# Two PSUM pools, other homes for the normalised tokens and token sums, and later places for chunk 0's down weights and chunk 2's normalisation, in a fused spectral mixer and GEGLU kernel

## The chip, the cores and the metric

The kernel runs as one program on one core of a Trainium2 chip. The metric is the device time of one execution in microseconds (us); lower is better. Five engines appear in the profile: TensorE (PE for matmuls, PEld for its weight loads), VectorE (DVE), ScalarE (ACT), GpSimd (POOL), and SyncE (SP), which issues the DMAs. [...]

## The reference, cut to what matters

```python
# x: 8192 tokens x 448; mod rows from silu(c) @ w_mod
sa, ca, ga, sb, cb, gb = ...
h = layernorm(x) * (1 + ca) + sa
x = x + ga * irfft2(softshrink(mlp2(rfft2(h))))   # complex MLP, block-diagonal (4 blocks of 112), relu between
h = layernorm(x) * (1 + cb) + sb
x = x + gb * ((gelu(h @ w_gate) * (h @ w_up)) @ w_down)   # w_gate, w_up: 448 x 1792; w_down: 1792 x 448
```

The Fourier transform runs along the 8192 tokens (the other transformed axis has length 1). All inputs and outputs are float32.

## The kernel before, in words

The program has three stages. Up to about 80 us it loads x, normalises it and does the first part of the transform. Up to about 372 us it does the rest of the transform, the block MLP and most of the inverse transform, and writes the result to a DRAM buffer `vd`. From there to the end it runs the last step of the inverse transform, the second normalisation and the feed-forward network (FFN), in 32 **chunks** of 256 tokens. The change lies in this third stage.

**Precision.** The large matmuls work in fp16, each operand as a high and a low half: ACT writes the high half (a cast or scaled copy), DVE or POOL the rest (`..._hi`, `..._lo`). Matmuls are grouped in Strassen-like products, for which sums of tokens, weights and activations are formed.

**Chunks 0 to 7, the standard chunks** (372 to 768 us). The 1792 hidden columns are 14 tiles. The loop over a chunk i runs k = 0 to 13, and `gate_up(i, k)` issues gate and up matmuls of tile k (line L1125), then gelu on ACT (L1161), the product of both on DVE (L1166, `x<-pgu,gel`), and at odd k four sums on POOL (L1174 to L1177, `sums`). `quantize` (L1185 on ACT, L1186 on DVE) makes the fp16 pair `ac` from it, one or two k later. After k == 2 of chunk i, `down(i-1)` runs: seven products of matmuls (L1198 to L1200), two banks in turn, with an epilogue on ACT, DVE and POOL (L1225 to L1245) between them; L1226 writes the first quarter of the output buffer `o`, and L1234 reads the bank that the next product but one needs. `down` has three places (`mid`, 0 to 2) at which other steps are put in.

**What a chunk needs beforehand.** For chunk i: the loads of `v` (from `vd`), `g` and the residual `xx`; `split_g`/`split_v` (POOL, ACT); `inverse` (PE, L1026); `residual` (DVE L1035, and L1036 on DVE up to chunk 2, on POOL from chunk 3); `stats2` (DVE, L1044); `rsqrt_part`, small DVE steps; `norm2(i, b)` for b = 0 and 1 (DVE, L1074 and L1075), which writes the normalised tokens `n` in a buffer `n2`; `pack_hi` (ACT, L1080) and `pack_lo` (POOL for i > 0, L1087 to L1089) into the buffer `pk`; and `transposes_dma` (SP, L1095), transposing DMAs from `pk` to `nt`, which the matmuls read. For chunk 0 PE transposes (L1107).

**Weights made meanwhile.** `down_hi(t)` (ACT, L947) and `down_lo(t)` (DVE, L951, two instructions) make the seven pairs `wd` of down weights from float32 loads (`load_d8`); pair 1 ahead of chunk 0's loop, pairs 2 to 6 inside it. During chunks 0 to 7 the weight forms of the later chunks are made too (L1532 to L1580).

**Chunks 8 to 31, the units** (768 us to the end). Each chunk is seven units u = 56 to 223. `period(u)` issues stages a to d of four units in flight (L1360), with copies out of PSUM on ACT (`copy_b`, L1388, `sb<-set`) and DVE steps. Between stage a of unit u and its stage b, PE waits for `copy_b`. A unit's matmuls write one of three sets of two PSUM banks. For chunk 8 and later, `token_sums` (DVE L1301 to L1307 and one copy on POOL, L1303) forms sums of `n` in a buffer `tf`, which `wpack_hi` (ACT, L1331) and `wpack_lo` (POOL, L1337) pack into `pk`; `wtransposes` then transposes. In the first units of chunk 8 the list `opening` gives the steps of chunk 9.

**The order of the work** is written by hand. Dictionaries name steps to be issued after `gate_up(i, k)`: `hooks` for chunks i < 6, `soon` for i = 6 and 7, `second` for chunk 2's preparation in chunk 1, `ahead` and `first` for single places (key i * 14 + k), `prep` for the weight forms.

**PSUM.** In the standard chunks one pool of eight banks holds four tags of two: `pc` (inverse, transposes of chunk 0, and one product of down), `pa`, `pb` (gate and up), `pd` (down). After chunk 7 the pool is closed and another opened, with the three sets and two banks for down; set0, which unit 56 uses, lies on the former banks of `pc`.

**SBUF homes.** The pool `cp` is opened for the third stage. Its first tiles are wd1 to wd6, then two x1 tiles, then `pk`; `n2` comes after further tiles. `o` (tag "o") is one buffer of the pool `cq`; token sums of chunk 8 use this same tag. `x8()` gives one of three buffers with the products of a tile pair.

Of the kernel before, what the change touches and what calls it, by code (L numbers as in the profile page):

```python
# [10 lines left out]
F32 = mybir.dt.float32  # L11
F32R = mybir.dt.float32r
F16 = mybir.dt.float16
# [6 lines left out]
D = 448  # L20
# [4 lines left out]
CB = 2  # L25
# [13 lines left out]
NXT = 25  # L39
LA = 2  # L40
NSTD = 8
# [8 lines left out]
def spectral_geglu(ctx, tc, x, w1, b1, w2, b2, wg, wu, wd, cvec, wmod, cf1, cs2, cmi, cgm, out):  # L50
# [11 lines left out]
    wk = [[dram.tile([128, 2, 2, 2, b - a, 128], F16, name=f"wk{t}{a}") for a, b in WPARTS] for t in range(NP)]  # L62

    cpool = ctx.enter_context(tc.tile_pool(name="cpool", bufs=1))
    pctx = ExitStack()
    psum = pctx.enter_context(tc.tile_pool(name="psum", bufs=2, space=bass.MemoryType.PSUM))

    def bank(tag, name):
        return psum.tile([128, 512], F32, tag=tag, name=name)

    eps = cpool.tile([128, 1], F32, name="eps")
    V.memset(eps, EPS)
# [254 lines left out]
    with ExitStack() as bctx:  # L327
# [617 lines left out]
        def down_hi(t):  # L945
            for r, k in zip(draws[t], (slice(0, 3), slice(3, 7))):
                S.activation(wds[t][:, 0, k], r, AF.Copy, scale=dsc[:, t : t + 1])  # L947
# [32 lines left out]
    with ExitStack() as cctx:  # L980
        cp = cctx.enter_context(tc.tile_pool(name="cp", bufs=1, side="right"))
        H = 128 * CB
        wds = wds + [cp.tile([128, 2, 7, HC], F16, name=f"wd{t}") for t in range(len(wds), NP)]
        x1s += [cp.tile([128, CB, D], F32, name=f"x1{n}") for n in (1, 2)]
        pkt = cp.tile([128, NXT * 128], F16, name="pk")
        pkts = [pkt]
        nts, acts, pgu, outs = {}, {}, {}, []

# [79 lines left out]

        def norm2(i, b):
            mvt, x1, r = nxt[i]["mv"], x1t[i], nxt[i]["r"][0]  # L1070
            if b == 0:
                nxt[i]["n"] = cp.tile([128, CB, D], F32, tag="n2", name="n2")
            n = nxt[i]["n"]
            V.scalar_tensor_tensor(n[:, b], x1[:, b], mvt[:, b, 0:1], cb_r, op0=ALU.subtract, op1=ALU.mult)  # L1074
            V.scalar_tensor_tensor(n[:, b], n[:, b], r[:, b : b + 1], sb_r, op0=ALU.mult, op1=ALU.add)  # L1075
# [215 lines left out]
        def token_sums(i, part):  # L1291

            n = nxt[i]["n"]
            if part == 0:
                nxt[i]["t"] = cq.tile([128, 2 * D], F32, tag="o", name="tf") if i < NSTD + 1 else cp2.tile([128, 2 * D], F32, tag="tf", name="tf")
            t = nxt[i]["t"]
            b11, b21, x0 = n[:, 0, 0:192], n[:, 0, 192:384], n[:, 0, 384:448]
            b12, b22, x1 = n[:, 1, 0:192], n[:, 1, 192:384], n[:, 1, 384:448]
            t1, t2, t3, t4 = (t[:, o : o + 192] for o in (0, 192, 384, 640))
            if part == 0:  # L1300
                V.tensor_tensor(t1, b12, b11, ALU.subtract)  # L1301
                V.tensor_tensor(t3, b22, b12, ALU.subtract)
                G.tensor_copy(t[:, 576:640], x1)  # L1303
            else:
                V.tensor_tensor(t2, b22, t1, ALU.subtract)
                V.tensor_tensor(t4, b21, t2, ALU.subtract)
                V.tensor_tensor(t[:, 832:896], x0, x1, ALU.subtract)  # L1307
# [197 lines left out]
            6: [(2, wpack_hi, [4]), (2, wpack_lo, [4]), (3, load_g)],  # L1505
        }

        def pack(i):
            pack_hi(i)
            pack_lo(i)  # L1510
# [122 lines left out]
        for n, k in enumerate((4, 7, 11, 13)):  # L1633
# [17 lines left out]
            0: [(inverse,), (residual,)],  # L1651
            1: [(stats2,), (rsqrt_part, 5)],
            2: [(rsqrt_part, 9)],
            "down": [(norm2, 0), (norm2, 1)],
            "down2": [(pack_hi,), (pack_lo,), (transposes_dma, range(1))],
        }

        soon = {
# [6 lines left out]
            9: [(2, rsqrt_part, 5)],  # L1665
            10: [(2, rsqrt_part, 9)],
            11: [(2, norm2, 0)],
            12: [(2, norm2, 1)],
        }

        ahead = {
# [2 lines left out]
        }  # L1674

        first = {
            0: [(down_hi, 2), (down_lo, 2), (load_d8, 4)],
            2: [(inverse, 1), (residual, 1), (stats2, 1), (rsqrt_part, 1, 9)],
            3: [(down_hi, 3)],
            4: [(pack_hi, 1), (pack_lo, 1), (down_lo, 3), (load_d8, 5)],  # L1680
            6: [(down_hi, 4)],
            7: [(down_lo, 4), (load_d8, 6)],
            9: [(down_hi, 5)],
            10: [(down_lo, 5)],
            12: [(down_hi, 6)],
# [30 lines left out]
        S.copy(gb_r, gb[:, :D])  # L1716
        for t0 in range(0, 7, 2):
            transposes(0, t0)
        down_hi(1)
        down_lo(1)  # L1720
        load_d8(3)
        V.tensor_scalar(gb_r, gb_r, ds_d, None, op0=ALU.mult)

        def store_out():
# [5 lines left out]
            return bank("pc" if q == 1 else "pd", "pdn")  # L1730

        def steps_std(i, n):
            for fn, *args in second[("down", None, "down2")[n]] if i == 1 and n != 1 else []:
                fn(2, *args)
            for fn, *args in prep.pop((i, f"m{n}"), []):
                fn(*args)

        for i in range(NSTD):
            if i == 1:
                cctx2.close()  # L1740
                cctx2 = ExitStack()
                cp2 = cctx2.enter_context(tc.tile_pool(name="cp3", bufs=1))
            for k in range(NFT):
                gate_up(i, k)
                for fn, *args in ahead.pop(i * NFT + k, []):
                    fn(*args)
                if k % 2 == 1 and i + k > 1:
                    quantize(*((i, k // 2 - 1) if k > 1 else (i - 1, NP - 1)))
                if i == 1:
                    for fn, *args in second.get(k, []):  # L1750
                        fn(2, *args)
                for fn, *args in prep.pop((i, k), []):
                    fn(*args)
                if k == 2 and i > 0:
                    down(i - 1, two_banks, lambda n: steps_std(i, n))
                    if i == 1:
                        transposes_dma(2, range(1, 2))
                if k == 4:
                    store_out()
                for fn, *args in first.pop(i * NFT + k, []):  # L1760
                    fn(*args)
                if (i, k) in ((0, 3), (1, 1)):
                    load_v(i + 2)
                    load_g(i + 2)
                if i == 1 and k == 3:
                    split_g(3)
                    split_v(3)
                if k == 9 and i > 0:
                    load_v(i + 3)
                    load_g(i + 3)  # L1770
                for d, fn, *args in (hooks if i < NSTD - 2 else soon).get(k, []):
                    if i == NSTD - 2 and k < 3 and d == 1:
                        continue
                    if i + d > 2 and i > 0 and (i, k) != (1, 1):
                        fn(i + d, *args)
        quantize(NSTD - 1, NP - 1)
        assert not prep and not first and not ahead
        cctx2.close()
        pctx.close()
        cp2 = cctx.enter_context(tc.tile_pool(name="wp", bufs=1))  # L1780
        psum2 = cctx.enter_context(tc.tile_pool(name="psum2", bufs=1, space=bass.MemoryType.PSUM))
        sets = [psum2.tile([128, 2, 512], F32, name=f"set{n}") for n in range(3)]
        sets = [sets[(n - U0) % 3] for n in range(3)]
        pdn = [psum2.tile([128, 512], F32, name=f"pdn{n}") for n in range(2)]
        pkts.append(cp2.tile([128, NXT * 128], F16, name="pk2"))
        x1s.append(cp2.tile([128, CB, D], F32, name="x13"))

        opening = {
            0: [
                (2, split_v),  # L1790
                (1, token_sums, 0),
                (1, token_sums, 1),
                (1, wpack_hi, [0, 1]),
# [105 lines left out]
```

## Time and profile before

| What | Value |
|---|---|
| median of 3 runs | 1904.54 us (1901.68 to 1906.47) |
| profiled execution | 1902.93 us |
| its span, from first to last recorded work | 1901.1 us |
| mean granted TensorE clock | 0.993 |
| DMA moved | 330.49 MB |

The page of the profile gives busy times per engine for the whole span. A line of a timeline gives the start, the duration, engine, source line, operation, "out<-in" with the shapes, and in square brackets the idle time of the engine just before, with what ended it. "x2" behind a line means that two instructions of the kind are taken together. A line of the waits gives the total, the number and the longest. PEclk is the clock granted to TensorE, 1.00 being full speed.

### The profile page before, as it was taken

The numbers are of one execution on the slowest core, as the hardware profiler recorded it, in microseconds if no ns is written. First come the engines' busy times: TensorE is split into PE (matmuls) and PEld (weight loads), VectorE is DVE, ScalarE is ACT, GpSimd is POOL, SyncE is SP. The second block draws the span as 40 slices with busy tenths as digits, with TensorE's granted clock in tenths as the row PEclk, the third lists the DMA queues.
The fourth block names the chain that finished last, engine by engine and source line by source line (L and its number), as shares of the span: only waits on it lengthen the run. The fifth ranks groups of instructions, "written<-read, shape, count | busy, mean of one in ns | idle before, by whom it ended". The sixth has DMA issues, their size and how long they took to land.

```text
span 1901.1 us, 56363 instructions
## 1 busy us (share of the span) xinstructions
PE 1855.4 (98%) x23332; PEld 1756.8 (92%) x23332; DVE 1428.5 (75%) x2888; ACT 996.1 (52%) x1844; POOL 1266.1 (67%) x1616
## 2 busy tenths in 40 slices
PE   7899999899999999999999999999999999999998
PEld 3599999878898998899999999999999999999998
DVE  8677788778766666677777777777777777777645
ACT  5687888653444444344555545455455454444443
POOL 3157654257777777577777777777777777777533
PEclk9999999999999999899999999999999999999999
DMA  9999777645444445866666656556666666666651
GB/s 353 317 295 260 205 177 197 181 136 143 103 102 102 102 102 119 252 171 178 177 177 172 167 167 167 167 167 167 172 177 175 169 174 178 173 177 174 155 152 55
DMA packets 380602, 330.49 MB, mean 174 GB/s; under 512 B 110772, under 2 KB 358712, under 8 KB 380344
## 3 DMA queue, kind: packets, MB, share of 16 engines
q1 hardware_dynamic: 380344, 326.87, 62.4%
q8 instruction: 183, 3.00, 0.6%
q14 instruction: 75, 0.61, 0.1%
HBM read 243.32 MB, written 60.10 MB: 160 GB/s over the span
## 4 chain that ended last, share of the span: by engine, by line
PE 78%; DVE 11%; DMA 4%; ACT 2%; POOL 2%; SPq 2%; issue 1%; ACTq 0%; DVEq 0%; POOLq 0%
PE set L1360 34%; PE pgu L1125 11%; PE pdn L1198 6%; PE pdn L1200 6%; PE pdn L1199 6%; PE set L1198 2%; PE set L1200 2%; PE set L1199 2%; PE ps L210 2%; DMA xt<-in_A_x 2%; DVE y L471 1%; DVE x L1413 1%; DMA raw<-in_B_w_up 1%; DVE c L1397 1%; DVE wk L826 1%
## 5 line engine op out<-in xcount | busy, mean ns | idle before, releaser
L1360 PE MATMUL set<-nt,wk 128*128 128x128 f16 x13104 | 746.4, 220 | 5.6 <-DVE x L1166 3.3
L1360 PEld LDWEIGHTS <-wk 128*128 128x128 f16 x13104 | 739.4, 98 | 10.7 <-issue 8.7
L1198 PE MATMUL pdn<-wd,ac 128*128 128x224 f16 x1218 | 316.5, 260 | 4.2 <-DVE u L1234 3.6
L1200 PE MATMUL pdn<-wd,ac 128*128 128x224 f16 x1218 | 316.3, 260 | 1.2 <-DVE ac L1435 1.2
L1199 PE MATMUL pdn<-wd,ac 128*128 128x224 f16 x1218 | 316.3, 260 | 0.0
L1125 PE MATMUL pgu<-nt,wk 128*128 128x256 f16 (+1 forms) x2464 | 267.5, 274 | 1.8 <-DVE x L1166 1.8
L1125 PEld LDWEIGHTS <-wk 128*128 128x128 f16 (+1 forms) x2464 | 225.8, 98 | 42.1 <-issue 16.4
L1409 ACT ACTIVATE gl<-c,dg 128x384 f32<-128x384 f32 x168 | 103.4, 616 | 254.3 <-DVE c L1403 253.2
L1435 DVE SCALAR_TENSOR_TENSOR ac<-x,sa_act,ac 128x896 f16<-128x896 f32 x168 | 212.3, 1264 | 14.7 <-ACT ac L1425 14.7
L1174 POOL TENSOR_TENSOR x<-x 128x128 f32<-128x128 f32 x223 | 129.5, 581 | 125.0 <-DVE x L1166 62.4
L1241 POOL TENSOR_TENSOR o<-u,p 128x224 f32<-128x224 f32 x32 | 21.1, 659 | 259.7 <-DVE u L1240 259.7
L1413 DVE TENSOR_TENSOR x<-c,gl 128x384 f32<-128x384 f32 x168 | 176.1, 1048 | 17.8 <-ACT gl L1409 17.7
L1425 ACT ACTIVATE ac<-x,sa_act 128x896 f16<-128x896 f32 x168 | 173.6, 1033 | 3.6 <-DVE x L1177 0.4
L1177 POOL TENSOR_TENSOR x<-x 128x128 f32<-128x128 f32 x223 | 170.8, 766 | 0.0
L1198 PEld LDWEIGHTS <-ac 128*128 128x128 f16 x1568 | 153.7, 98 | 5.9 <-issue 4.8
L1199 PEld LDWEIGHTS <-ac 128*128 128x128 f16 x1568 | 153.8, 98 | 4.2 <-issue 3.9
L1200 PEld LDWEIGHTS <-ac 128*128 128x128 f16 x1568 | 153.7, 98 | 1.9 <-DVE ac L1435 1.7
L1176 POOL TENSOR_TENSOR x<-x 128x128 f32<-128x128 f32 x223 | 149.3, 670 | 0.0
L1397 DVE TENSOR_TENSOR c<-set,sb 128x512 f32<-128x512 f32 x168 | 115.0, 684 | 38.5 <-PE set L1360 38.5
L1161 ACT ACTIVATE gel<-pgu,dg 128x256 f32<-128x256 f32 x112 | 49.8, 471 | 165.6 <-PE pgu L1125 155.1
L1175 POOL TENSOR_TENSOR x<-x 128x128 f32<-128x128 f32 x223 | 119.1, 534 | 17.5
L471 DVE SCALAR_TENSOR_TENSOR y<-pm,t 64x224 f32<-64x224 f32 x256 | 99.5, 389 | 39.0 <-ACT t L463 35.1
(324 smaller groups left out, 3986.0 us busy)
## 6 DMA issues: line engine op xcount, KB each, us to landing
wk<-wk SPq DMA_DIRECT2D x76, 1024.0 KB, 5.5
wk<-wk SPq DMA_DIRECT2D x76, 768.0 KB
tr<-td SPq DMA_DIRECT2D x64, 224.0 KB, 4.6
vd<-us SPq DMA_DIRECT2D x64, 224.0 KB, 3.1
xx<-in_A_x SPq DMA_DIRECT2D x32, 448.0 KB, 6.1
v<-vd SPq DMA_DIRECT2D x63, 224.0 KB, 5.8
out<-x SPq DMA_DIRECT2D x31, 448.0 KB, 2.7
xt<-in_A_x SPq DMA_DIRECT2D x15, 896.0 KB, 18.2
```

The costliest lines, as they stand in the source:

```text
L1125: T.matmul(pgu[i, t, q][:, pr * H : (pr + 1) * H], ws[rows, n, w, tw], nts[i][rows, tn, :], start=start, stop=stop, skip_group_check=True,)
L1174: e.tensor_tensor(s1, a21, a22, ALU.add)
L1176: e.tensor_tensor(s3, a11, a21, ALU.subtract)
L1177: e.tensor_tensor(s4, a12, s2, ALU.subtract)
L1198: T.matmul(ps, ac[:, 0, ka], w[:, 0, kb], start=n == 0, stop=False)
L1199: T.matmul(ps, ac[:, 0, ka], w[:, 1, kb], start=False, stop=False)
L1200: T.matmul(ps, ac[:, 1, ka], w[:, 0, kb], start=False, stop=n == NP - 1)
L1360: T.matmul(ps2[:, pr, reg * 128 : reg * 128 + 128], slot[:, pr, hl, wt, :], nt[:, xt, :], start=start and j == 0, stop=j == len(terms) - 1 ...
L1397: V.tensor_tensor(c[:, :, 1:3, :], p[:, :, 0:256].rearrange("p g (r c) -> p g r c", r=2), b[:, :, 0:128].rearrange("p g (o c) -> p g o c", ...
L1413: V.tensor_tensor(xs[u][:, 1::3, :], cts.pop(u)[:, 1], gls.pop(u), ALU.mult)
L1425: S.activation(ac[:, 0], xs[u][:, 0:7], AF.Copy, scale=sa_act[:, t : t + 1])
L1435: V.scalar_tensor_tensor(ac[:, 1], xs.pop(u)[:, 0:7], sa_act[:, t : t + 1], ac[:, 0], op0=ALU.mult, op1=ALU.subtract)
```

## The change

The change has six parts, and all of them move or rename: no matmul is added or taken away, and the arithmetic is the same.

1. The tag `pc` gets a PSUM pool of its own, on the right side, and set0 a pool of its own in its place; both old pools are closed after chunk 7 as before.
2. `norm2(9, 1)` goes from k = 12 of chunk 7 to `opening[0]`, ahead of chunk 9's token sums.
3. The token sums of chunk 8 lie in an `x8` buffer and no longer in tag "o".
4. `n2` and `pk` are the first tiles of the pool `cp`, ahead of the down weights.
5. `down_hi`, `down_lo` and `load_d8` of pair 1 go from ahead of chunk 0's loop to its k = 1, and the following pairs each one place back.
6. Chunk 2's `norm2`, packing and transposes go from the places in down(0) to k = 3, 4, 5 and 6 of chunk 1.

```diff
-    pctx = ExitStack()
+    pctx, pcctx = ExitStack(), ExitStack()
+    psumc = pcctx.enter_context(tc.tile_pool(name="psumc", bufs=2, space=bass.MemoryType.PSUM, side="right"))
     psum = pctx.enter_context(tc.tile_pool(name="psum", bufs=2, space=bass.MemoryType.PSUM))
     def bank(tag, name):
-        return psum.tile([128, 512], F32, tag=tag, name=name)
+        return (psumc if tag == "pc" else psum).tile([128, 512], F32, tag=tag, name=name)
...
         H = 128 * CB
+        nxt[0]["n"] = cp.tile([128, CB, D], F32, tag="n2", name="n2")
+        pkt = cp.tile([128, NXT * 128], F16, name="pk")
         wds = wds + [cp.tile([128, 2, 7, HC], F16, name=f"wd{t}") for t in range(len(wds), NP)]
         x1s += [cp.tile([128, CB, D], F32, name=f"x1{n}") for n in (1, 2)]
-        pkt = cp.tile([128, NXT * 128], F16, name="pk")
...
         def norm2(i, b):
-            if b == 0:
+            if b == 0 and i > 0:
                 nxt[i]["n"] = cp.tile([128, CB, D], F32, tag="n2", name="n2")
...
             if part == 0:
-                nxt[i]["t"] = cq.tile([128, 2 * D], F32, tag="o", name="tf") if i < NSTD + 1 else cp2.tile([128, 2 * D], F32, tag="tf", name="tf")
+                nxt[i]["t"] = x8().rearrange("p n c -> p (n c)")[:, : 2 * D] if i == NSTD else cp2.tile([128, 2 * D], F32, tag="tf", name="tf")
...
+        def last_norm(i):
+            if i == NSTD:
+                norm2(i, 1)
...
         second = {
             0: [(inverse,), (residual,)],
             1: [(stats2,), (rsqrt_part, 5)],
             2: [(rsqrt_part, 9)],
-            "down": [(norm2, 0), (norm2, 1)],
-            "down2": [(pack_hi,), (pack_lo,), (transposes_dma, range(1))],
+            3: [(norm2, 0)],
+            4: [(norm2, 1)],
+            5: [(pack_hi,), (pack_lo,)],
+            6: [(transposes_dma,)],
         }
         soon = {
...
-            12: [(2, norm2, 1)],
+            12: [(2, last_norm)],
         }
         first = {
-            0: [(down_hi, 2), (down_lo, 2), (load_d8, 4)],
+            1: [(down_hi, 1), (down_lo, 1), (load_d8, 3)],
             2: [(inverse, 1), (residual, 1), (stats2, 1), (rsqrt_part, 1, 9)],
-            3: [(down_hi, 3)],
-            4: [(pack_hi, 1), (pack_lo, 1), (down_lo, 3), (load_d8, 5)],
-            6: [(down_hi, 4)],
-            7: [(down_lo, 4), (load_d8, 6)],
+            3: [(down_hi, 2)],
+            4: [(pack_hi, 1), (pack_lo, 1), (down_lo, 2), (load_d8, 4)],
+            5: [(down_hi, 3)],
+            6: [(down_lo, 3), (load_d8, 5)],
+            7: [(down_hi, 4)],
+            8: [(down_lo, 4), (load_d8, 6)],
             9: [(down_hi, 5)],
             10: [(down_lo, 5)],
...
         for t0 in range(0, 7, 2):
             transposes(0, t0)
-        down_hi(1)
-        down_lo(1)
-        load_d8(3)
         V.tensor_scalar(gb_r, gb_r, ds_d, None, op0=ALU.mult)
...
         pctx.close()
+        pcctx.close()
         cp2 = cctx.enter_context(tc.tile_pool(name="wp", bufs=1))
         psum2 = cctx.enter_context(tc.tile_pool(name="psum2", bufs=1, space=bass.MemoryType.PSUM))
-        sets = [psum2.tile([128, 2, 512], F32, name=f"set{n}") for n in range(3)]
+        psum3 = cctx.enter_context(tc.tile_pool(name="psum3", bufs=1, space=bass.MemoryType.PSUM, side="right"))
+        sets = [(psum2 if n else psum3).tile([128, 2, 512], F32, name=f"set{n}") for n in range(3)]
+        pdn = [psum2.tile([128, 512], F32, name=f"pdn{n}") for n in range(2)]
         sets = [sets[(n - U0) % 3] for n in range(3)]
-        pdn = [psum2.tile([128, 512], F32, name=f"pdn{n}") for n in range(2)]
...
         opening = {
             0: [
                 (2, split_v),
+                (1, norm2, 1),
                 (1, token_sums, 0),
                 (1, token_sums, 1),
```

More of the change, by code (lines that the diff above doesn't have):

```diff
@@ L1732, in steps_std @@
         def steps_std(i, n):
-            for fn, *args in second[("down", None, "down2")[n]] if i == 1 and n != 1 else []:
-                fn(2, *args)
             for fn, *args in prep.pop((i, f"m{n}"), []):
@@ L1755, in spectral_geglu @@
                     down(i - 1, two_banks, lambda n: steps_std(i, n))
-                    if i == 1:
-                        transposes_dma(2, range(1, 2))
                 if k == 4:
```

## The prediction

> **What bounds the kernel now.** I read the page's busy times first, then TensorE's (PE's) waits by stretch, then the timeline around each of its waits in the stretches that the diff touches, then the granted clock there.
>
> ```profile
> PE 1855.4 (98%) x23332; PEld 1756.8 (92%) x23332; DVE 1428.5 (75%) x2888; ACT 996.1 (52%) x1844; POOL 1266.1 (67%) x1616
> ```
>
> PE is busy 98% of the span. The change touches no matmul, so it can gain only what PE waits, or runs at half clock, where the diff acts. Waits of PE at 700 to 770 us, then its two longest on DVE at 360 to 460 us (us in total, times, longest us):
>
> ```profile
> PE set L1360 <- DVE x L1166: 3.3, 1, 3.3
> PE pdn L1198 <- DVE u L1234: 2.1, 1, 2.1
> ```
>
> ```profile
> PE pgu L1125 <- DVE x L1166: 1.8, 1, 1.8
> PE pdn L1198 <- DVE u L1234: 1.4, 1, 1.4
> ```
>
> These four are the change's ground. Around three of them, by windows of 3.4 us and one of 10.2 (busy us and count of each engine, then PEclk, the granted clock):
>
> ```profile
> core 0: us, PE busy (x) PEld busy (x) DVE busy (x) ACT busy (x) POOL busy (x), PEclk, DMA share, GB/s
> 402.60:406.00 3.40, 1.77 (x17) 1.44 (x15) 3.40 (x5) 2.61 (x4) 2.32 (x3) 1.00 0.09 10
> 730.40:733.80 3.40, 1.27 (x14) 1.17 (x12) 3.26 (x5) 0.00 (x0) 2.79 (x3) 0.98 0.00 0
> 733.80:737.20 3.40, 3.40 (x21) 2.78 (x20) 2.14 (x4) 0.00 (x0) 1.61 (x2) 0.52 0.63 130
> 764.40:767.80 3.40, 1.28 (x12) 0.99 (x11) 3.36 (x5) 0.84 (x2) 2.92 (x4) 1.00 1.08 365
> 767.80:778.00 10.20, 8.29 (x77) 8.13 (x77) 6.61 (x10) 4.32 (x9) 6.43 (x9) 0.50 1.10 340
> ```
>
> After the windows with 1.27 and 1.28 us of work the clock was halved, after the one with 1.77 us it was not. So a stall also costs the work that then runs at half clock: 3.40 x (1 - 0.52) = 1.6 us after the first, and in the second, with PE back to back from 773.28 to 778.0, 4.7 x 0.5 = 2.4 us.
>
> **Token sums of chunk 8 in another buffer.** They were in a buffer that the epilogue of down(6) also needs:
>
> ```profile
> 726.92 2.17 POOL L1337 TENSOR_TENSOR pk<-tf,pk 128x128 f16<-128x128 f32 x3
> ```
>
> ```profile
> 724.63 0.32 ACT L1225 COPY p<-pdn 128x224 f32<-128x224 f32 x1
> ```
>
> ```profile
> 729.12 0.39 DVE L1226 TENSOR_TENSOR o<-pdn,p 128x224 f32<-128x224 f32 x1 [5.49 <-POOL pk L1337]
> 729.43 2.84 DVE L1571 SCALAR_TENSOR_TENSOR ws<-wr,sww,ws 128x128 f16<-128x128 f32 x2
> 732.19 0.38 DVE L1234 TENSOR_TENSOR u<-pdn,p 128x224 f32<-128x224 f32 x1
> ```
>
> L1226 waits until GpSimd (POOL) has packed the low halves of those sums; behind it in VectorE's (DVE's) order stand the weight quantisation (2.84) and L1234, which frees the bank for PE's next product. In an x8 buffer, one of three, whose former reader L1186 is long done by then, that wait goes: L1226 needs only its product and the copy p at 724.63, so it comes near 725.0, 4.1 us earlier, and L1234 with it near 728.1, well ahead of 730.5, when PE wants the bank (L1234's end 732.6 less the 2.1). Nothing else is late next: PE's own product takes the wait's place. With the window full, the half clock goes too: -2.1 - 1.6 = **-3.7** (end: -2.1, if the clock's drop hung on where its window fell). [...]
>
> **Two PSUM pools, and norm2(9,1) later.** The first unit's banks, set0, lie on those of the old tag pc. DVE's, POOL's, ScalarE's (ACT's) and PE's timelines:
>
> ```profile
> 754.62 1.15 DVE L1035 TENSOR_TENSOR x<-pi,ga_r 128x448 f32<-128x448 f32 x2
> ```
>
> ```profile
> 766.93 0.95 DVE L1074 SCALAR_TENSOR_TENSOR n<-x,cmv,cb_r 128x448 f32<-128x448 f32 x1
> 767.91 0.69 DVE L1075 SCALAR_TENSOR_TENSOR n<-n,rcy,sb_r 128x448 f32<-128x448 f32 x1
> 768.52 0.42 DVE L1166 TENSOR_TENSOR x<-pgu,gel 128x256 f32<-128x256 f32 x1
> ```
>
> ```profile
> 769.01 1.29 POOL L1174 TENSOR_TENSOR x<-x 128x128 f32<-128x128 f32 x1 [1.61 <-DVE x L1166]
> ```
>
> ```profile
> 771.70 1.04 ACT L1185 ACTIVATE ac<-x,sa_act 128x896 f16<-128x896 f32 x1 [3.23 <-POOL x L1177]
> 772.65 0.58 ACT L1388 COPY sb<-set 128x512 f32<-128x512 f32 x1
> ```
>
> ```profile
> 768.99 3.57 PE L1360 MATMUL set<-nt,wk 128*128 128x128 f16 x32 [3.31 <-DVE x L1166]
> 773.28 10.89 PE L1360 MATMUL set<-nt,wk 128*128 128x128 f16 x152 [0.72 <-ACT sb L1388]
> ```
>
> The last read of pc's banks is the 754.62 row, yet the 32 matmuls wait until 768.99 for L1166 on another tag: a new pool waits for the whole of the closed one. With pc in a pool of its own they start at once, near 765.45. But the next matmuls wait for the copy sb, and ACT takes it only behind L1185, which waits for POOL's four sums, which wait for that same L1166. So the 3.3 us of wait mostly turn into a wait for sb. What moves sb is norm2(9,1), taken from ahead of L1166: L1166 goes from 768.52 to about 766.93, 1.59 earlier, and POOL to ACT to PE with it: 773.28 becomes about 771.75, -1.5. Before that PE has a gap of some 4.5 us after its 32 matmuls, so I keep a half clock of 2.1 against 2.4 (-0.2): **-1.7**. Ends: -0.6 (norm2's 1.64 us delays the copies in its new place by 1.1) and -2.5 (clock nearly kept). In its new place, ahead of unit 0's token sums, norm2(9,1) holds back DVE's L1301 and through it ACT's packing; transposes of chunk 9 come only two units later, so I count nothing; uncovered it would cost its 1.64.
>
> **Homes of n2 and pk.**
>
> ```profile
> 376.25 0.69 DVE L1074 SCALAR_TENSOR_TENSOR n<-x,mv,cb_r 128x448 f32<-128x448 f32 x1 [0.74 <-DMA g<-cgm]
> ```
>
> The first write of n waited 0.74 for something that its inputs don't explain: memory of the stage before. Other addresses in the same closed pool, which set0 shows to be waited for as a whole: **0** (end: -0.74).
>
> **Chunk 0's down weights later.** All steps of down_hi and down_lo keep their order; one pair (1) goes from ahead of chunk 0 to k=1, the rest one place back.
>
> ```profile
> 388.06 1.15 DVE L951 SCALAR_TENSOR_TENSOR wd<-dr,dsc,wd 128x896 f16<-128x896 f32 x1 [1.80 <-ACT wd L947]
> ```
>
> ```profile
> 403.61 2.15 DVE L951 SCALAR_TENSOR_TENSOR wd<-dr,dsc,wd 128x672 f16<-128x672 f32 x2
> 405.68 0.74 DVE L1166 TENSOR_TENSOR x<-pgu,gel 128x256 f32<-128x256 f32 x2
> 406.35 2.12 DVE L1186 SCALAR_TENSOR_TENSOR ac<-x,sa_act,ac 128x896 f16<-128x896 f32 x1
> 408.39 0.77 DVE L1166 TENSOR_TENSOR x<-pgu,gel 128x256 f32<-128x256 f32 x2
> ```
>
> ```profile
> 410.60 0.33 PEld L1125 LDWEIGHTS <-wk 64*128 64x128 f16 x8 [0.21 <-issue]
> ```
>
> Pair 1 stood where DVE idled anyway (1.80 before the row shown), and now stands in DVE's closed stretch up to 406, where a pair costs about 2.1. One pair less stands there at the end (each is a place later), so L1166 at 405.68, for which PE waits 1.8, comes only 0.3 to 0.4 later: +0.4. But the pair formerly at 403.61 now stands ahead of the L1166 of 408.39, which would end at 409.2 + 0.4 + 2.15 = 411.7 against 410.6 + 0.4 for the halves that need it: +0.65. The load ahead of pair 5 now queues on SyncE behind chunk 1's transposes: +0.3. Together **+1.3** (ends: 0, if DVE catches up at k=2 to 7, and +2.15, a whole pair).
>
> **Chunk 2's normalisation from the middle of down(0) to k=3 to 6 of chunk 1.** DVE at 436 to 439.5 us by lines, then the part of the three packing steps on POOL in a window (columns as above):
>
> ```profile
> L1074 DVE SCALAR_TENSOR_TENSOR n<-x,cmv,cb_r 128x448 f32<-128x448 f32 x2 | 1.8, 900 | 0.0
> L1075 DVE SCALAR_TENSOR_TENSOR n<-n,rcy,sb_r 128x448 f32<-128x448 f32 x2 | 1.4, 685 | 0.1
> ```
>
> ```profile
> 440.00:443.20 3.20, 0.00 (x0) 0.00 (x0) 0.00 (x0) 0.35 (x1) 2.60 (x3) 1.00 0.20 41
> ```
>
> ```profile
> 463.64 2.54 POOL L1036 TENSOR_TENSOR x<-x,xx 128x448 f32<-128x448 f32 x2 [1.03 <-DVE x L1035]
> ```
>
> ```profile
> 467.94 8.63 PEld L1125 LDWEIGHTS <-wk 128*128 128x128 f16 x80 [0.21 <-issue]
> 476.78 0.11 PEld L1125 LDWEIGHTS <-wk 64*128 64x128 f16 x4 [0.21 <-issue]
> 477.12 0.20 PEld L1125 LDWEIGHTS <-wk 64*128 64x128 f16 x4 [0.23 <-issue]
> ```
>
> Those 3.2 us of DVE stood ahead of the L1234 for which PE waited 1.4: gone, **-1.4**. The packing (2.6 on POOL) moves to k=5, ahead of residual(3) at 463.64, where POOL had 1.03 of idle time: residual is 2.6 - 1.0 = 1.6 later at an even load, 0.85 to 2.0 with POOL's neighbours shifting. DVE's statistics of chunk 3 wait for it, and then DVE runs almost closed up to the L1166 that frees the bank for the halves at 476.78, which have no more than 0.23 of idle time: of the delay I let 0.9 reach PE. With +1.3: this region **+0.8** (ends -1.4, both absorbed; +2.7: 2.15 + 2.0 - 1.4).
>
> **Sum.** -3.7 - 1.7 + 0.8 = -4.6. The profiled execution took 1902.93 (span 1901.1), the median of the runs is 1904.54, 1.6 above it; so 1898.3 there, and 1899.9, rounded **1900.0**, as a median. About 0.3% (5.7 us) is what a measurement of this kernel can tell from no change: faster means below 1898.8, slower above 1910.3.
>
> **Rivals.** (a) *More gain*: the delays at chunk 0 and chunk 1 are absorbed. For it: POOL is busy 67%, DVE 75%, and both idle elsewhere between chunks. Against: the rows above are closed just there. -3.7 - 2.5 - 1.4 = -7.6: 1896.9.
> (b) *Less*: every end against: -2.1 - 0.6 + 2.7 = 0: 1904.5. For it: one run's clock proves little. [...]
> (c) *The split frees nothing* (set0 still waits for the other pool, as its sets share one hand-over): the 32 matmuls start with L1166, and behind them the sb path stays as late as before but for the clock: 0 in place of -1.7: 1901.7.
> (d) *Slower*: chunk 2's transposes land late.
>
> ```profile
> 440.88 5.16 SPq L1095 DMA_TRANSPOSE nt<-pk x4
> ```
>
> They now issue at k=6, from about 461 to 466, instead of at 440.88, and chunk 2's first matmul is due 40 loads after 467.94, at 467.94 + 40 x 0.108 = 472.3. It decides from a landing after 472.3: each us later is one of PE, and from some 2 us on a half clock (2.1) comes on top. To be slower it must cost 1910.3 - 1900.0 = 10.3, of which 8.2 stall: a landing at 480.5. At 482: 1900.0 + 9.7 + 2.1 = 1911.8. For it: they pass behind nothing but share the queue with two stores and the loads of weights; against: four took 5.16 to issue, and landing 14 us after that has no row.
>
> **How the numbers follow.** The forecast 0.50 (its own range 1897.5 to 1902.5, a fourth of it below 1898.8), (a) 0.33, (b) 0.09, (c) 0.03, (d) 0.05. Faster 0.33 + 0.12 = 0.45; within 0.3% 0.38 + 0.09 + 0.03 = 0.50; slower 0.05. Range: down to 1895.5, through most of (a); up to 1904.5, the end of (b); outside stay (d) and about 0.1 below.
>
> **What would show it.** Right: L1226 in down(6) without a wait on POOL's L1337, the 2.1 us wait gone and a clock near 1.0 at 733 to 738; the first 32 of L1360 right behind the last gate-and-up matmul and a wait for sb of about 4 us behind them; PE's 1.4 at down(0) gone; a longer wait at k=8 and a new one at k=9 of chunk 0. Wrong: PE going straight on from unit 0's first half to the second (E worth up to 8), no halves late at chunks 0 and 2 (then (a)), or a wait for nt at chunk 2's first matmul (then (d)).

## The result and the profile after

| | before | after |
|---|---|---|
| median of 14 runs each | 1904.42 us (1901.48 to 1907.32) | 1902.56 us (1900.26 to 1907.54) |
| ratio, 95% interval | | 0.9991 (0.9982 to 0.9999) |
| profiled execution, its span | 1902.93, 1901.1 us | 1900.89, 1899.1 us |

The change makes the kernel about 1.9 us faster, within the 0.3% that were taken as no change, and inside the range of 1895.5 to 1904.5. The forecast was 1900.0, a gain of 4.5: less than half of it came. Line numbers of the changed kernel are 1 to 6 higher than before: L1168 is the old L1166, L1236 the old L1234, L1362 the old L1360, L1390 the copy sb.

The page's busy times, then the waits of PE that changed at 360 to 490 us and at 700 to 790 us (total, times, longest):

```profile
PE 1853.8 (98%) x23332; PEld 1754.4 (92%) x23332; DVE 1429.7 (75%) x2888; ACT 994.8 (52%) x1844; POOL 1265.3 (67%) x1616
```

```profile
PE pgu L1127 <- DVE x L1168: 4.8, 4, 2.4
PE pi L1028 <- POOL v L116: 1.0, 1, 1.0
```

```profile
PE set L1362 <- ACT sb L1390: 4.2, 1, 4.2
```

The 2.1 us wait in down(6), the 1.4 us wait in down(0) and the 3.3 us wait ahead of unit 56 are gone. In their place stand a 4.2 us wait for sb, where 0.7 was, and at gate and up 4.8 us where 1.8 were. The windows of after around the places that changed (columns as in the windows of before):

```profile
core 0: us, PE busy (x) PEld busy (x) DVE busy (x) ACT busy (x) POOL busy (x), PEclk, DMA share, GB/s
467.20:470.60 3.40, 0.99 (x12) 0.47 (x10) 2.92 (x7) 0.73 (x1) 2.15 (x2) 1.00 0.45 107
470.60:474.00 3.40, 3.40 (x21) 2.37 (x21) 3.16 (x11) 1.53 (x3) 2.58 (x4) 0.60 1.20 209
729.60:733.00 3.40, 3.40 (x38) 3.40 (x36) 1.44 (x3) 2.42 (x6) 3.32 (x8) 1.00 0.00 0
733.00:736.40 3.40, 3.40 (x38) 3.40 (x37) 1.74 (x3) 0.00 (x0) 3.40 (x3) 1.00 0.00 0
766.20:769.60 3.40, 1.83 (x33) 1.71 (x31) 2.19 (x5) 1.52 (x2) 3.31 (x7) 1.00 1.07 364
769.60:773.00 3.40, 0.77 (x8) 0.77 (x8) 1.98 (x3) 2.33 (x3) 1.03 (x1) 0.80 1.09 344
773.00:776.40 3.40, 3.40 (x46) 3.40 (x44) 3.33 (x4) 1.40 (x6) 2.76 (x3) 0.70 1.10 342
```

At 730 to 736 us, where before had a half clock, PE is full at a clock of 1.00. At 467 to 474 us, where before ran through, there is a new hole (0.99 us of work in 3.4) and a half clock behind it (0.60).

The instructions of both kernels can be set side by side by the start of POOL's first sum (L1174, L1176) of the same tile pair. Differences of these starts, and of PE's first product of down(7) (785.41 us before, 783.45 after), give the time by stage:

| Stage | after against before |
|---|---|
| up to the first write of n (376.25 before) | -0.1 us |
| chunk 0, up to chunk 1's first pair | +1.6 |
| chunk 1 and 2 | +3.0 |
| chunks 3 to 7, up to the last pair but one | -4.0 |
| from there to down(7) | -2.5 |
| sum | -2.0, as the spans have it |

From chunk 3 to down(6) the difference stays at 4.50 within 0.03 us.

### The profile page after: what moved, and what is told of

Its sections match the earlier page's. It is cut to its first block, busy times and chain, and to the rows that moved or that the text cites. A ratio compares the mean times of both kernels' runs of the same rounds, so it can differ in the third digit from the quotient of the medians.

```text
span 1899.1 us, 56360 instructions
## 1 busy us (share of the span) xinstructions
PE 1853.8 (98%) x23332; PEld 1754.4 (92%) x23332; DVE 1429.7 (75%) x2888; ACT 994.8 (52%) x1844; POOL 1265.3 (67%) x1616
## 4 chain that ended last, share of the span: by engine, by line
PE 80%; DVE 8%; DMA 4%; ACT 3%; SPq 2%; issue 2%; POOL 1%; ACTq 0%; DVEq 0%; POOLq 0%
PE set L1362 37%; PE pgu L1127 11%; PE pdn L1202 6%; PE pdn L1200 6%; PE pdn L1201 6%; PE ps L211 2%; DVE y L472 2%; PE set L1201 2%; PE set L1202 2%; PE set L1200 2%; DVE wk L827 1%; PE set L1472 1%; ACT th L114 1%; DVE st L172 1%; DMA tr<-td 0%
## 5 line engine op out<-in xcount | busy, mean ns | idle before, releaser
L1362 PE MATMUL set<-nt,wk 128*128 128x128 f16 x13104 | 743.9, 220 | 5.6 <-ACT sb L1390 4.2
L1362 PEld LDWEIGHTS <-wk 128*128 128x128 f16 x13104 | 736.9, 98 | 10.5 <-issue 8.2
L1176 POOL TENSOR_TENSOR x<-x 128x128 f32<-128x128 f32 x223 | 131.4, 589 | 124.1 <-DVE x L1168 85.4
```

Source lines behind the costliest of these rows:

```text
L1176: e.tensor_tensor(s1, a21, a22, ALU.add)
L1362: T.matmul(ps2[:, pr, reg * 128 : reg * 128 + 128], slot[:, pr, hl, wt, :], nt[:, xt, :], start=start and j == 0, stop=j == len(terms) - 1 ...
```

## The experiments

The same three differences were taken for every kernel below, each against the kernel before: **A** from the first write of n to the last pair of chunk 2, **B** from there to chunk 7's last pair but one, **C** from there to the first product of down(7). A, B and C come from one profiled execution each; that of split_norm was the fastest of its 11, those of gains_only and combined the slowest of theirs. Where no interval stands, only these differences and the waits are read. Lines in the rows below are shifted by a few against the kernel before, as in after.

| Kernel | A | B | C | ratio (interval) |
|---|---|---|---|---|
| after | +4.6 | -4.0 | -2.5 | 0.9991 (0.9982 to 0.9999) |
| gains_only | +0.8 | -4.0 | -1.6 | 0.9970 (0.9958 to 0.9982) |
| norm_undone | +1.6 | -4.0 | -1.2 | |
| weights_undone | +3.2 | -4.0 | -2.2 | |
| no_pack_lo2 | +2.1 | -4.0 | -1.2 | |
| no_norm2_2 | +1.5 | -4.0 | -1.1 | |
| pools_only | +0.1 | -1.7 | -0.5 | |
| norm9_only | -0.2 | -0.1 | -2.9 | |
| x8_only | 0.0 | -4.0 | -2.3 | |
| late_quant | +0.4 | -4.0 | -1.1 | 0.9975 (0.9966 to 0.9984) |
| split_norm | +0.3 | -4.0 | -2.9 | 0.9978 (0.9969 to 0.9987) |
| combined | +2.3 | -4.0 | -4.7 | 0.9957 (0.9943 to 0.9971) |
| final | +2.0 | -4.0 | -4.9 | 0.9959 (0.9946 to 0.9973) |

The sum of A, B and C is not the whole gain. Near 1880 us, behind all three, the clock was halved for another 3.4 us in the executions of gains_only, no_pack_lo2, x8_only, late_quant and split_norm, and their spans end 1.5 to 1.7 us later than their difference at down(7) would have it.

**gains_only**: the changed kernel with the two parts of chunks 0 to 2 undone.

```diff
-            1: [(down_hi, 1), (down_lo, 1), (load_d8, 3)],
+            0: [(down_hi, 2), (down_lo, 2), (load_d8, 4)],
...
+        down_hi(1)
+        down_lo(1)
+        load_d8(3)
...
-            3: [(norm2, 0)],
-            4: [(norm2, 1)],
-            5: [(pack_hi,), (pack_lo,)],
-            6: [(transposes_dma,)],
+            "down": [(norm2, 0), (norm2, 1)],
+            "down2": [(pack_hi,), (pack_lo,), (transposes_dma, range(1))],
```

> The changed kernel with two parts undone: chunk 0's down weights and chunk 2's normalisation stand at their old places; the two pools, norm2(9,1), the homes and the token sums stay changed. Theory: the two undone parts cost 1.5 us (chunk 0) and 3.0 us (chunk 1: 1.4 saved at down(0); 0.4, 2.4 of a new wait and some 1.6 of half clock lost). Then this kernel is faster than the one before by 3.9 + 2.2 = 6.1 us, a ratio near 0.9968, and PE shows at 360 to 490 us the waits of before (1.8 at gate and up, 1.4 at down(0)). Rival: the other homes of n2 and pk delay chunks 0 to 2; then a wait at gate and up of over 2 us stays and the gain is under 4 us.

Median 1897.52 against 1903.10 us, 5.6 us faster, where 6.1 were expected. PE's waits at 360 to 490 us are 1.4 at gate and up and 1.7 in down(0), where the kernel before had 1.8 and 1.4. So the two parts that were undone cost about 4 us, and the rival, a cost of the homes of n2 and pk, falls. In the changed kernel n's first write still waits 0.69 us, where it waited 0.74:

```profile
376.16 0.68 DVE L1076 SCALAR_TENSOR_TENSOR n<-x,mv,cb_r 128x448 f32<-128x448 f32 x1 [0.69 <-DMA g<-cgm]
```

**norm_undone and weights_undone**: each undoes one of the two blocks of gains_only.

> The changed kernel with chunk 2's normalisation back in down(0); the down weights stay late. Theory: the 2.4 us wait at gate and up in chunk 1 and the half clock behind it are gone, the 1.4 us wait at down(0) is back, and chunk 2 ends about 1.5 us later than in the kernel before, not 4.5. Rival: the late down weights push chunk 1's steps as well; then a wait of over 1 us at gate and up in chunk 1 stays and chunk 2 ends over 2.5 us later.

> The changed kernel with only chunk 0's down weights back at their old places; chunk 2's normalisation stays at k=3 to 6 of chunk 1. Theory: the two parts add up, so chunk 2 ends 3.0 us later than in the kernel before (4.5 with both): the 2.4 us wait at gate and up in chunk 1 and the half clock stay, chunk 0 shows one wait of 1.8. Rival: the late weights make the wait in chunk 1; then it is under 1 us and chunk 2 ends less than 1.5 us late.

With the normalisation undone, A is +1.6, with the weights undone +3.2, together 4.8 against 4.6 with both: the parts add up, as expected. Without the moved normalisation the 2.4 us wait is gone and down(0)'s 1.4 us wait is back; with it the 2.4 us wait stands, whatever the weights do. Both rivals fall.

**no_pack_lo2 and no_norm2_2**: which of the moved steps makes the wait of 2.4 us? Each of the two kernels leaves one of them out for chunk 2.

```diff
 # no_pack_lo2, in pack_lo
+                if i == 2:
+                    continue
...
 # no_norm2_2, in norm2
+            if i == 2:
+                nxt[2]["n"] = nxt[1]["n"]
+                return
```

> The changed kernel without the three low-half packing steps of chunk 2 on POOL (left out of the computation); all else stays. Theory POOL (the packing, 2.3 us ahead of sums(1,3) and residual(3), makes chunk 3's statistics late): residual(3) starts near 464.0 in place of 466.8, and the 2.4 us wait at gate and up in chunk 1 is gone or under 0.4. Rival DVE (the moved norm2 itself makes DVE late, so that L1037, which residual(3) needs, starts at 465.6 anyway): residual(3) starts at 466.0 or later, at most 0.8 earlier, and a wait of 1.6 to 2.4 stays.

> The changed kernel without the four norm2 steps of chunk 2 on DVE (left out of the computation, chunk 1's normalised tokens are packed again); packing and transposes stay at k=5 and 6. Theory POOL: the wait at gate and up in chunk 1 stays over 1.6 us. Rival DVE: it is gone or under 0.6, and residual(3) starts by 465.0.

PE's wait at gate and up at 445 to 470 us and the start of residual(3) on POOL, first without the packing, then without norm2:

```profile
PE pgu L1129 <- DVE x L1170: 1.1, 1, 1.1
```

```profile
465.71 1.14 POOL L1038 TENSOR_TENSOR x<-x,xx 128x448 f32<-128x448 f32 x1 [0.30 <-DVE x L1037]
```

```profile
PE pgu L1130 <- DVE x L1171: 0.9, 1, 0.9
```

```profile
465.03 1.13 POOL L1038 TENSOR_TENSOR x<-x,xx 128x448 f32<-128x448 f32 x1
```

Neither theory holds alone. residual(3) starts at 466.81 in the changed kernel; without the packing it starts 1.1 earlier and then waits for DVE's L1037, without norm2 1.8 earlier. Each leaves a wait of about 1 us. In neither does the clock fall: A drops by 2.5 and 3.1 us, of which the wait itself is 1.3 and 1.5.

**pools_only, norm9_only, x8_only**: one part alone on the kernel before (the edits are those of the change).

> The kernel before with the two PSUM pools alone. Theory: the first 32 matmuls of unit 56 start with no wait, but stage b waits for sb as late as before, near 773.3 on that timeline, a wait of 5.5 to 6.2 us in one piece: nothing gained, -0.3 to +0.5 us. Rival: the pools carry the gain; then stage b comes 2 us earlier.

> The kernel before with norm2(9,1) moved behind unit 56 alone; one PSUM pool. Theory: the last L1166 of chunk 7 comes 1.6 us earlier, and with it the start of unit 56, sb and stage b: -1.5 us up to unit 57, with the half clock about as long as before. Rival: without the second pool the gain is under 0.5 us.

> The kernel before with the token sums of chunk 8 in an x8 buffer alone. Theory: the 2.1 us wait in down(6) is gone and the clock stays at 1.0 behind it: -3.7 to -3.9 us from chunk 7's start on. Rival (the half clock there was a chance of the window, or belongs to another gap): -2.1 us.

PE's waits at 700 to 800 us of the three, in this order:

```profile
PE set L1361 <- ACT sb L1389: 5.8, 1, 5.8
PE pdn L1199 <- DVE u L1235: 2.1, 1, 2.1
```

```profile
PE set L1360 <- ACT sb L1388: 3.2, 2, 2.3
PE pdn L1198 <- DVE u L1234: 2.1, 1, 2.1
PE set L1360 <- DVE x L1166: 1.7, 1, 1.7
```

```profile
PE set L1360 <- DVE x L1166: 3.3, 1, 3.3
PE set L1360 <- ACT sb L1388: 0.9, 1, 0.9
```

Stage b of unit 56, reckoned from chunk 7's last pair but one, starts 0.02 us earlier with the pools alone, 1.61 earlier with norm2(9,1) alone, 1.60 earlier with both. So the second pool gains nothing and norm2(9,1) all, as the prediction's sum had it. The clock was not as expected: in norm9_only it is 1.00 from 764 to 782 us, where a half clock about as long as before was expected, and C is -2.9. x8_only takes the 2.1 us wait away and shows B at -4.0, as expected. What was not expected is the rest of C. x8_only changes nothing behind chunk 7, its stage b is not earlier, and yet down(7) comes 2.3 us earlier than in the kernel before: the granted clock is 0.51 from 765.3 to 768.7 us and 0.99 behind that, while before had 0.50 up to 778.0. And pools_only keeps the 2.1 us wait of down(6) with B at -1.7: the clock did not fall behind it.

```profile
729.70:733.10 3.40, 1.70 (x18) 1.54 (x17) 3.11 (x4) 0.00 (x0) 3.40 (x4) 1.00 0.00 0
733.10:736.50 3.40, 3.01 (x32) 3.01 (x32) 3.26 (x8) 0.00 (x0) 1.99 (x2) 1.00 0.20 42
```

**late_quant**: gains_only, with the last quantisation of chunk 7 issued behind unit 56, so that sb no longer stands behind it on ACT.

```diff
-        quantize(NSTD - 1, NP - 1)
...
             period(u)
+            if u == U0:
+                quantize(NSTD - 1, NP - 1)
```

> The changed kernel with the down weights and chunk 2's normalisation at their old places (as in gains_only), and the quantisation of chunk 7's last tile pair issued behind unit 56 and not ahead of it. Theory: what holds unit 56's stage b is the copy sb standing on ACT behind that quantisation; behind the pair before it (ACT at about 768.0 to 769.0 on the changed kernel's timeline) the copy comes 2.6 us earlier, so the 4.2 us wait falls to about 1.6, and with the clock kept 1 to 2 us more are saved: -2.6 to -4.9 us against gains_only, a ratio near 0.995 against the kernel before. Rival: the late quantisation delays down(7) or the steps of chunk 9 on DVE; then unit 57 or 58 waits and the gain is under 1 us.

1898.43 us, ratio 0.9975: no gain over gains_only. PE's waits at 700 to 800 us, and ACT at the second of them:

```profile
PE set L1362 <- ACT sb L1390: 4.2, 2, 2.7
```

```profile
773.05 0.41 ACT L1333 CAST pk<-n 128x256 f16<-128x256 f32 x1 [2.67 <-DVE n L1077]
773.37 0.58 ACT L1390 COPY sb<-set 128x512 f32<-128x512 f32 x1
```

The first wait fell to 1.5 us as the theory had it, and unit 57's sb then waited 2.7: on ACT it stands behind a cast of chunk 9's tokens, which waits for norm2(9,1), the step that the change had put there. The gain turned into a new wait one unit later.

**split_norm**: late_quant, and chunk 2's normalisation split around down(0)'s epilogue, its low halves packed on DVE.

```diff
-            "down": [(norm2, 0), (norm2, 1)],
-            "down2": [(pack_hi,), (pack_lo,), (transposes_dma, range(1))],
+            "down": [(norm2, 0)],
+            "down3": [(norm2, 1), (pack_hi,)],
...
             p3 = product(i, banks(6), 6)
+            if i == 0:
+                mid(3)
...
-                e = V if i == 0 else G
+                e = V if i in (0, 2) else G
...
-                        transposes_dma(2, range(1, 2))
+                        pack_lo(2)
+                        transposes_dma(2)
```

> The kernel late_quant, and of chunk 2's normalisation in down(0) only the first half ahead of L1234's bank; the second half and the packing of the high halves behind the epilogue's last use of u, the low halves on DVE and no longer on POOL, all transposes after down(0). Theory: the 1.4 to 1.7 us wait in down(0) goes, and as DVE is idle there and POOL gets no packing, no new wait comes: -1.4 us or somewhat more against late_quant, a ratio near 0.994. Rival: DVE's first L1166 steps of chunk 1 come late, and a wait at gate and up of 1 us or more takes the place of the one removed.

1899.31 us, ratio 0.9978. The wait in down(0) is gone and none comes at gate and up, but the inverse of chunk 3 waits 1.7 us for POOL's split_v(3) where it waited 0.6, since POOL's chain of steps behind down(0) ends no earlier. So the wait is given back there: A is +0.3, against +0.4 in late_quant. C is -2.9 against -1.1, because in this execution the clock stayed at 1.00 around unit 56; the medians show no such gain.

**combined**: split_norm, norm2(9,1) back at its old place, the quantisation behind unit 57, split_v(3) in the middle of down(0).

```diff
+            if i == 1 and n == 1:
+                split_g(3)
+                split_v(3)
...
-            12: [(2, last_norm)],
+            12: [(2, norm2, 1)],
...
-            if u == U0:
+            if u == U0 + 1:
                 quantize(NSTD - 1, NP - 1)
```

> The kernel split_norm with three more edits. (1) norm2(9,1) is back at k=12 of chunk 7: in late_quant it stood on DVE ahead of ACT's packing, behind which the copy sb of unit 57 waited 2.7 us. (2) The quantisation of chunk 7's last pair stands behind unit 57, not 56. (3) split_g(3) and split_v(3) stand in the middle of down(0), where POOL idles 4.4 us, and not at k=3 of chunk 1, where PE waited 1.7 us for them. Theory: at unit 56 a wait of about 1.5 us stays and the one for unit 57's sb goes, and the 1.7 us wait of the inverse in chunk 1 goes: PE's waits from 420 to 800 us fall from 6.5 to 2 us or less, and the time to about 1895, a ratio near 0.995. Rival: the steps moved wait on the same engines and the waits only change places; then they stay over 4.5 us and the ratio above 0.997.

1896.96 us, ratio 0.9957. C improves to -4.7, with the clock at 1.00 there as in split_norm: the first two edits work. The third does not. PE's two longest waits from 420 to 800 us, DVE's step ahead of L1236, and POOL beside it:

```profile
PE pdn L1200 <- DVE u L1236: 2.5, 1, 2.5
PE set L1364 <- ACT sb L1392: 1.5, 1, 1.5
```

```profile
440.13 2.42 DVE L1575 SCALAR_TENSOR_TENSOR ws<-wr,sww,ws 128x384 f16<-128x384 f32 x1
```

```profile
439.69 2.45 POOL L116 TENSOR_TENSOR v<-v,vh 128x896 fp32r<-128x896 f32 x1
```

The wait for split_v went, and a wait of 2.5 us in down(0) came: PE's waits at 420 to 800 us sum to 5.4 us, over the rival's 4.5 and far from the theory's 2. Of them 1.2 us are a new wait in the units, for a load of weights (`wk`).

**final**: combined without that third edit.

> The kernel combined without its third edit: split_g(3) and split_v(3) stand again at k=3 of chunk 1. Theory: in combined the 2.45 us of split_v on POOL stretched one DVE step beside it from 0.6 to 2.4 us, and L1236 behind that step held PE for 2.5 us and cost the clock. Without the edit that wait and its half clock go, the 1.7 us wait of the inverse comes back: -1 to -2.5 us up to chunk 2's end, a ratio near 0.995 against the kernel before. Rival: the step is long for another reason; then the wait of over 2 us in down(0) stays.

1896.73 us, ratio 0.9959. The 2.5 us wait is gone, and the same L1575 takes 0.61 us with POOL idle beside it:

```profile
439.09 0.61 DVE L1575 SCALAR_TENSOR_TENSOR ws<-wr,sww,ws 128x384 f16<-128x384 f32 x1
```

The gain up to chunk 2's end is 0.3 us and not 1 to 2.5, because the clock now fell behind the 1.7 us wait of the inverse. split_norm has the same steps there, the same wait (453.72 to 455.40 us; 454.43 to 456.11 in final), and no fall. The windows below are laid in steps of 3.41 us from the changes of the clock in the same trace (see the last section), three of split_norm and then two of final:

```profile
450.94:454.35 3.41, 2.66 (x21) 1.90 (x18) 3.38 (x6) 2.04 (x4) 3.41 (x5) 1.00 0.46 159
454.35:457.76 3.41, 2.36 (x17) 1.96 (x18) 3.41 (x3) 0.57 (x1) 3.33 (x3) 1.00 0.95 217
457.76:461.18 3.42, 3.42 (x36) 2.71 (x34) 2.20 (x4) 1.72 (x4) 3.04 (x7) 1.00 0.32 75
```

```profile
453.40:456.81 3.41, 1.59 (x7) 0.99 (x6) 3.41 (x3) 1.26 (x3) 3.41 (x3) 1.00 0.59 123
456.81:460.22 3.41, 3.41 (x17) 2.15 (x17) 3.06 (x4) 0.61 (x1) 3.25 (x5) 0.50 0.79 192
```

In split_norm the wait lies across two windows, and the emptier still has 2.36 us of matmul work. In final all of it lies in one, which is left with 1.59.

combined and final are faster than the kernel before by 6.7 and 7.6 us in their medians, and by their ratios than the changed kernel by about 6; between the two no difference is measured.

## Why the prediction was right, and where a step was not

The time lies in the range, but the sum was 2.6 us too hopeful. Its three terms, -3.7, -1.7 and +0.8, came out as -4.0, -2.5 and +4.6. So the large miss is in chunks 0 to 2, and a clock that fell for a shorter time than forecast behind chunk 7 hid about 0.7 us of it by luck.

**Token sums: right.** -3.7 forecast, -4.0 measured in the execution of every kernel with this part. Without its wait for POOL, L1228 waits for ACT's copy p and L1236 for PE's own product:

```profile
729.48 0.39 DVE L1228 TENSOR_TENSOR o<-pdn,p 128x224 f32<-128x224 f32 x1 [1.35 <-ACT p L1227]
...
733.04 0.39 DVE L1236 TENSOR_TENSOR u<-pdn,p 128x224 f32<-128x224 f32 x1 [1.99 <-PE pdn L1202]
```

The end of -2.1, kept for a clock that falls by chance, is real too: pools_only has the wait without the fall, and there the part would be worth 4.0 - 1.7 = 2.3 us.

**Two pools and norm2(9,1): the mechanism was right, the clock term was not one number.** -1.7 forecast, -2.5 in this execution. The 32 matmuls start at once and PE then waits for sb, behind POOL and ACT:

```profile
766.08 1.95 PE L1362 MATMUL set<-nt,wk 128*128 128x128 f16 x32
772.23 10.10 PE L1362 MATMUL set<-nt,wk 128*128 128x128 f16 x154 [4.20 <-ACT sb L1390]
```

```profile
770.66 1.04 ACT L1187 ACTIVATE ac<-x,sa_act 128x896 f16<-128x896 f32 x1 [1.63 <-POOL x L1179]
771.61 0.56 ACT L1390 COPY sb<-set 128x512 f32<-128x512 f32 x1
```

Of C, 1.6 us are the wait (-1.5 forecast). The other 0.9 is clock, where -0.2 was forecast, and it varies from execution to execution. Of the six kernels with this part as in the change and the quantisation at its old place, after and weights_undone have the clock halved for 3.4 us and show C at -2.5 and -2.2; the four others have it halved for 6.8 us and show -1.1 to -1.6. The unchanged stage shows 0 with 10.2 us of half clock (before) and -2.3 with 3.4 (x8_only). How often each length comes is not settled by single executions.

**Homes: nothing against it.** 0 was forecast, and the wait ahead of n's first write changed by 0.05 us; no kernel has this part alone.

**Down weights: right**, +1.3 forecast, +1.6 found. A longer wait at k=8 and a new one at the halves behind it come as named; then there are more of the same kind. The 0.3 for a late load of weights is not seen in this execution, where neither ACT nor DVE waits for a DMA at 400 to 425 us; no_pack_lo2, with the weights at the same places, shows such a wait of 0.3 on ACT. PE's rows:

```profile
406.49 4.85 PE L1127 MATMUL pgu<-nt,wk 128*128 128x256 f16 x43 [1.94 <-DVE x L1168]
411.62 4.96 PE L1127 MATMUL pgu<-nt,wk 64*128 64x256 f16 x45 [0.28 <-DVE x L1168]
416.75 1.47 PE L1127 MATMUL pgu<-nt,wk 128*128 128x256 f16 x12 [0.17 <-DVE x L1168]
```

**Chunk 2's normalisation: wrong in size.** The sum held -0.5 for it (1.4 saved, 0.9 lost); measured is +3.0: 1.4 saved in down(0), then 0.4 lost at the inverse, 2.4 in a new wait at the halves and 1.6 of clock behind that wait. The failed step is "of the delay I let 0.9 reach PE". The timelines of POOL, DVE and PE's weight loads of the changed kernel:

```profile
462.39 1.64 POOL L1091 TENSOR_TENSOR pk<-n,pk 128x768 f16<-128x768 f32 x1
463.99 1.30 POOL L1176 TENSOR_TENSOR x<-x 128x128 f32<-128x128 f32 x1
...
466.81 1.13 POOL L1038 TENSOR_TENSOR x<-x,xx 128x448 f32<-128x448 f32 x1
```

```profile
469.38 0.63 DVE L1046 BATCH_NORM_STATS2 cst<-x 128x6 f32<-128x448 f32 x1 [0.48 <-POOL x L1038]
469.93 0.30 DVE L1049 BATCH_NORM_AGGREGATE cmv<-cst 128x2 f32<-128x6 f32 x2
470.14 0.39 DVE L1168 TENSOR_TENSOR x<-pgu,gel 128x256 f32<-128x256 f32 x1
```

```profile
467.78 0.12 PEld L1127 LDWEIGHTS <-wk 64*128 64x128 f16 x4 [0.21 <-issue]
470.59 0.20 PEld L1127 LDWEIGHTS <-wk 64*128 64x128 f16 x4 [2.69 <-issue]
```

Three things were missed. First, the 1.4 saved and the delay were added up as if they had nothing to do with each other. The delay came in the size forecast (1.6, ends 0.85 to 2.0): counted from chunk 1's first pair, residual(3) starts 1.65 us later than in the kernel before, and 1.57 in weights_undone. But PE, without its wait in down(0) and after the 0.4 at the inverse, was by then 1.0 us ahead, and the chain on POOL and DVE had not moved up with it. So PE waited for the delay and for its own gain as well, 2.7 us less the little idle time that was there. That the 1.6 fits is in part luck: only the packing was priced, while norm2, now on DVE in chunk 1, delays the same chain through L1037, as the two kernels with one of them left out show. Second, the chain meets PE one pair earlier than was thought: statistics of chunk 3, then at once the L1168 that frees the bank for the halves at 470.59, with nothing to spare. Third, the wait cost the clock as well, 1.6 us more; the sum priced the clock where the change removed waits and not where it made one.

The rivals: (a), more gain, needed the delays absorbed and they were not. (b), every end against (1904.5): its +2.7 for chunks 0 to 2 was still too small (+4.6), and its other ends did not come. (c), the split frees nothing (1901.7), lies nearest to the measured 1902.56, but by luck: its mechanism is false, as the 32 matmuls start without a wait in pools_only and after; they are only worth nothing here. (d) did not happen: chunk 2's transposes were issued from 462.2 to 468.2 us, and PE waits for none.

## What to carry to other kernels

A step moved out of one engine's critical stretch is paid for where it lands on every engine that it uses: follow each of its parts to the next bank that PE wants, and where that row has no idle time, count the delay in full and the clock behind it (here 2.4 us of wait and 1.6 of clock). A wait that is removed ahead of such a place is kept as a gain only if what PE waits for next moves up too. When an early start is gained for the first half of a stage, look for what releases the second half (here a copy behind a quantisation on ACT); moving the earlier work off that path, and not the start, is what gains. Where a trace has a gap like the two here, of 1.7 and 2.1 us, each of which cost the clock in one kernel and not in another, give its clock as a chance.

## What the runs showed of the hardware

**The clock falls or not behind the same gap.** A wait of 1.7 us at the same place was followed by a clock of 0.50 in final and of 1.00 in split_norm, one of 2.1 us by 0.52 in before and by 1.00 in pools_only. In each of the 14 traces the changes of the clock lie whole multiples of 3.41 us apart: in before it is halved from 733.65 to 737.06 us and from 767.79 to 778.02. Where these multiples fall in the program differs between executions: the wait of the inverse begins 2.78 us behind one in split_norm (453.72, 450.94) and 1.03 behind one in final (454.43, 453.40). Windows laid at them sort the cases. Between 400 and 800 us, with the clock at 1.00 in the window itself, every window with at most 1.40 us of matmul work was followed by a half clock, and none with more than 1.60; between these, final's 1.59 was followed by one and five windows with 1.48 to 1.57 were not. Near 1880 us five windows with 1.64 to 1.74 were followed by one too, so these runs give no exact bound. In final and in before, where the clock fell, all of the gap lies in one window (453.40 to 456.81 us with 1.59 us of work, 730.24 to 733.65 with 1.28); in split_norm, where it did not, the gap lies across two (2.66 and 2.36). That this decides whether a gap costs the clock is an estimate from these cases. The gap of 1.7 us cost final 3.41 x 0.50 = 1.7 us of clock, and cost split_norm nothing.

**Two DVE steps took longer beside a step on POOL.** A DVE step of 0.61 us (final) took 2.42 in combined, beside a subtraction of 2.45 us on POOL that had begun before it. In the changed kernel the second half of norm2(2), moved to k=4, met the same POOL step and took 2.17; in the kernel before it took 0.68 with POOL idle (437.98 us):

```profile
453.44 2.17 DVE L1076 SCALAR_TENSOR_TENSOR n<-x,cmv,cb_r 128x448 f32<-128x448 f32 x1
```

```profile
452.73 2.40 POOL L116 TENSOR_TENSOR v<-v,vh 128x896 fp32r<-128x896 f32 x1
```

In both cases DVE's step ends shortly after POOL's: 0.5 us after it in the one (455.61 and 455.13) and 0.4 in the other (442.55 and 442.14). As both are less than the 0.68 and 0.61 that the steps take alone, a part of each may have run beside POOL's. So a price taken from a row where POOL was idle was too low by 1.49 us (2.17 less 0.68) and 1.81 (2.42 less 0.61) in these two places.
